# A short convolution on two 64-row halves, with a new order for the whole kernel

## The chip, the cores and the metric

One core of a Trainium2 chip. The metric is the time of one execution in microseconds on the device, the median of several runs. A run of the profiler gives one execution with its rows for every instruction; its span is the time from the first to the last of them, and its own time is a little more than the span.

The engines are TensorE (PE, with its weight loads PEld), VectorE (DVE), ScalarE (ACT), GpSimd (POOL) and SyncE (SP), which here only issues DMAs. All of them run their instructions in the order of the program.

## The reference

All inputs are bf16; one batch, S = 2048 positions, D = 640 channels, F = 1728.

```python
def A(q, k, v, shift_k, ssm_k, ssm_D):        # q is layernorm(x)
    k_shift = sum over t in 0..3 of  k_pad[:, t:t + S, :] * shift_k[:, 3 - t]
    kv = k_shift * v
    y = causal convolution of kv with ssm_k over all S positions, per channel   # by FFT
    return q * (y + kv * ssm_D)

x = A_q
h  = x + A(layernorm(x), A_k, A_v, A_shift_k, A_ssm_k, A_ssm_D)
h2 = h + (silu(n @ w_gate) * (n @ w_up)) @ w_down     # n = layernorm(h)
```

So every position of k is mixed with the three before it, channel by channel ("taps"), then comes the long convolution, then a gated feed-forward net.

## The kernel before

The positions are cut into four blocks of 512. Position p * 4 + r of a block lies in partition p and "row" r (R = 4 rows of 128 partitions). Channels come in KT = 5 chunks of 128. The long convolution is done with a transform of length 1024 per block: matrices WF (forward, L345 in `forward`) and WI (inverse, L703 in `inverse`) on TensorE, and products of spectra on VectorE (`mac`, L560 for a first product, L587 and L588 for those that add). Block j takes the spectra X0..Xj of kv and the windows H0..Hj of the filter, whose spectra are called G. The result is multiplied with the normalized x and added (L717, L723), normalized again (L598, L645, L648), turned (L743 and copies L745, or a transposing DMA L736) and given to the feed-forward net `ffn` of that block: gate and up projections (L789 and L824), silu and product (L807 to L834), down projection (L856), and the store.

The short convolution, where the change lies: k of block 0 is loaded plainly (L506) and turned on TensorE by `turned_k` (L519, with copies L521 by ScalarE or VectorE), k of the others by transposing DMAs (L508). After that, channels lie in the partitions. In `kv_of`, for each row r, TensorE runs 20 pairs of weight load and matmul (L540): 5 chunks times 4 taps, the weights being turned k (128 channels by 128 positions) and the moving operand a diagonal matrix of 128 columns with that tap of the channels. The four sums of a row lie in PSUM in the layout of v. For block 0 VectorE multiplies with v straight out of PSUM (L545, four products of 640 columns); for the others ScalarE copies (L547) and VectorE multiplies in place (L548), or VectorE does both at once. The matrix `diag`, 20 diagonals of 128 columns, is made by one VectorE product (L892) from the identity and the loaded taps `tapw` (L882 in the rows of SP's issues).

The order of all work on each engine is fixed ahead by a planner, `Plan`. Each operation has an engine, a cost in nanoseconds, its reads and writes, and a priority. The planner takes the operations as its own model of time lets them start, those of lower priority number first. The priority of each stage is a base (10 for each block) plus an offset of the table PLACE: "k1" is the short convolution of block 1, "X1" its transform, "m11" a product, "f0" a feed-forward block, "Lk1", "Lv1", "Lg1", "Lx1" are loads, "LWF", "LWI", "Lm" (the table of negatives for the transforms, "minus"), "Ld", "Lw1" (`wd`, the weights of the down projection) and "Lwg" (the first feed-forward weights) too. SP's loads are one queue in the order of the plan. Buffers are few: SLOTS gives one for x, two for `ld` (v and g, which take turns in the order of their creation), two for `kT` (k), eight for spectra.

Of the kernel before, what the change touches and what calls it, by code (L numbers as in the profile page):

```python
# [19 lines left out]
P = 128  # L20
# [4 lines left out]
EPS = 1e-5  # L25
NEWTON = ((1.68191274, 0.70395035), (1.50000037, 0.50000005))
KT = D // P
NC_FULL = 13
NCH = NC_FULL + 1
NGRP = 7  # L30
NH = 320
ADDLO, ADDMAC, ADDWIN, ADDH, LEAD = ('G1',), (), (), (2,), {}
PAD = 16
DIRECT, ACTLN, ACTKV, ACTLN2 = ('inv0', 'G0', 'G1'), 1, 1, (2, 3)
LN1DVE, LN2POOL, HTURN = (2,), (), (2, 1)
GTURN = (3, 1, 2)
SUM = {'i3': 'four', 'G1': 'four', 'X1': 'four', 'X0': 'four'}
ADDP = {(3, 2): ((0, 1),), (2, 2): ((0, 1),), (2, 1): ((0, 0),)}
WAIT = {'dve': 450, 'act': 450, 'pe': 150}
PLACE = {"G0": 26.0, "G1": -15.5, "G2": -8.0, "G3": 12.0, "LWF": -13.5, "LWI": 16.0, "Ld": 20.0, "Lg0": -24.0,  # L40
# [8 lines left out]
SLOTS = {"S": 8, "scr": 4, "x": 1, "ld": 2, "kT": 2, "t4": 2, "hT": 1, "tT": 1, "wgu": 2, "row": 3, "o": 2,  # L49
         "sg": 2, "ps_c": 2, "ps_f": 2, "sm": 6}  # L50
SPLIT = ((0,), (1,))
# [36 lines left out]
class Plan:  # L88
# [4 lines left out]
    def __init__(self, slots, in_turn=()):  # L93
        self.ops, self.slots = [], slots
        self.turn = {t: [] for t in in_turn}
        self.at = {}
        self.all = 0.0

    def line(self, block, name, at, **own):

        at += PLACE.get(name, 0.0)
        self.block, self.all, self.at = block, at, {e: p + PLACE.get(name + e, 0.0) for e, p in own.items()}

    def add(self, eng, ns, fn, reads=(), writes=(), holds=(), other=None):


        deps, bufs = set(), list(holds)
        for acc, is_w in [(a, False) for a in reads] + [(a, True) for a in writes]:
            b, part = acc if isinstance(acc, tuple) else (acc, None)
            if b not in bufs:  # L110
                bufs.append(b)
            for op, p2, w2 in b.log:
                if (is_w or w2) and (part is None or p2 is None or part == p2
                                     or isinstance(part, frozenset) and isinstance(p2, frozenset) and part & p2):
                    deps.add(op)
        op = Op(len(self.ops), eng, ns, fn, self.at.get(eng, self.all), bufs, deps)
        op.other = other
        for acc, is_w in [(a, False) for a in reads] + [(a, True) for a in writes]:
            b, part = acc if isinstance(acc, tuple) else (acc, None)
            b.log.append((op, part, is_w))  # L120
        for b in bufs:
            b.left += 1
        self.ops.append(op)
        return op

    def schedule(self):
# [10 lines left out]
        while todo:  # L137
            found = []
            for op in todo:
                ready = 0.0  # L140
                ok = True
                want = {}
                for b in op.bufs:
                    if b.tag is not None and b.at is None:
                        if b.tag in self.turn and self.turn[b.tag][0] is not b:
                            ok = False
                            break
                        n = want[b.tag] = want.get(b.tag, 0) + 1
                        if len(idle[b.tag]) < n:
                            ok = False  # L150
                            break
                        ready = max(ready, sorted(idle[b.tag])[n - 1][0])
                    elif b.tag is not None:
                        ready = max(ready, b.since)
                if not ok:
                    continue
                for way, late in [((op.eng, op.ns, op.fn), 0.0)] + ([(op.other, 1e3)] if op.other else []):
                    at = max(ready, free.get(self.QUEUE.get(way[0], way[0]), 0.0))
                    for d in op.deps:
                        if d.eng != way[0] or d.eng in self.ISSUE:  # L160
                            at = max(at, d.end + self.LAND.get(d.eng, 0))
                    found.append(((at, op.prio + late, op.n), op, way))
            best = min(found, key=lambda f: f[0]) if found else None
            if best:
                until = best[0][0] + WAIT.get(best[2][0], 0)
                best = min((f for f in found if f[2][0] == best[2][0] and f[0][0] <= until and (f[0][1] <= best[0][1] - 5 or f is best)),
                           key=lambda f: (f[0][1] // 5, f[0][0], f[0]))
            assert best is not None, "the plan is stuck"
            (start, _, _), op, way = best
            if way is op.other and op.rest:  # L170
                op.rest.ns, op.rest.fn = 0, None
# [33 lines left out]
def kernel(ctx: ExitStack, tc: tile.TileContext, A_q, A_k, A_v, A_shift_k, A_ssm_k, A_ssm_D, B_x,  # L205
# [80 lines left out]
    WF = fixed([P, R, 4, P], BF16, "WF")  # L286
    WI = fixed([P, 4, R, P], BF16, "WI")
    tapw = fixed([P, KT, 4], BF16, "tapw")
    diag = fixed([P, KT * 4, P], BF16, "diag")
    wd = fixed([P, NCH, D], BF16, "wd")  # L290
    blanks = Buf(None)

# [209 lines left out]
    def load_k(j):  # L502

        kT = new("kT")
        if j == 0:
            load(MB, lambda: nc.sync.dma_start(out=plain(kT), in_=block(kk, j)), [kT])  # L506
        for r in range(R) if j else ():
            plan.add("turn", MB / 4 / 300.0, lambda r=r: nc.sync.dma_start(  # L508
                out=ap(kT)[:, :, r, PAD:], in_=block(kk, j)[:, r, :], transpose=True), [], [(kT, r)])
        return kT  # L510

    def turned_k(k):
        kT = new("kT")
        for r in range(R):
            pt = conv_ps()

            def tr(r=r, pt=pt):
                for c in range(KT):
                    nc.tensor.transpose(turned(pt)[:, c * P:(c + 1) * P], plain(k)[:, r, c * P:(c + 1) * P], ap(ident))  # L519
            pe(290, tr, [k, ident], [pt], [kT])  # L520
            evict(lambda copy, r=r, pt=pt: copy(  # L521
                ap(kT)[:, :, r, PAD:], turned(pt)[:, 0:D].rearrange("p (c t) -> p c t", c=KT)), [pt], [(kT, r)], other=490)
        return kT
# [1 line left out]
    def kv_of(j, kT, before, v):  # L525
# [4 lines left out]
            plan.add("pool", 900, lambda: nc.gpsimd.tensor_copy(ap(kT)[:, :, :, PAD - 1:PAD], ap(before)[:, :, :, PAD + P - 1:]),  # L530
                     [(before, r) for r in range(R)], [(kT, "halo")])
        kv = new("t4")
        for r in range(R):
            ps = conv_ps()

            def mm(r=r, ps=ps):
                for c in range(KT):
                    for t in range(4):
                        q, off = (r - t, PAD) if r >= t else (r - t + 4, PAD - 1)
                        nc.tensor.matmul(line(ap(ps))[:, c * P:(c + 1) * P], ap(kT)[:, c, q, off:off + P],  # L540
                                         ap(diag)[:, 4 * c + t, :], start=(t == 0), stop=(t == 3))
            pe(1130, mm, [kT, diag], [ps], [kv])

            def straight(r=r, ps=ps):
                nc.vector.tensor_mul(ap(kv)[:, r, :], line(ap(ps)), rd(v)[:, r, :])  # L545
            if plan.block >= ACTKV:
                op = plan.add("act", 700, lambda r=r, ps=ps: nc.scalar.copy(ap(kv)[:, r, :], line(ap(ps))), [ps, v], [(kv, r)], (), ("dve", 820, straight))  # L547
                op.rest = dve(490, lambda r=r: nc.vector.tensor_mul(ap(kv)[:, r, :], ap(kv)[:, r, :], rd(v)[:, r, :]), [v], [(kv, r)])  # L548
            else:
                dve(820, straight, [ps, v], [(kv, r)])  # L550
        return kv

    def mac(A, X, H, first, pieces=((0, 1),), adds=()):
# [23 lines left out]
        for xs, hs, dst, f in ((0, 0, 0, nc.vector.tensor_add), (0, 1, 1, nc.vector.tensor_add),  # L577
# [1 line left out]
            b = new("scr")  # L579

            if (xs, hs) in adds:
                dve(1490, lambda b=b, xs=xs, hs=hs: nc.vector.tensor_mul(flat2(b), X.part(xs), H.part(hs)), [X.at(xs), H.at(hs)], [b], [A.b])
                add_into(lambda dst=dst: A.part(dst), lambda b=b: flat2(b), [b], [A.at(dst)])
                continue

# [162 lines left out]

    def load_w(gi):
        w = new("wgu")  # L750
        was = plan.all
        if plan.block == 0 and gi < 2:
            plan.all = PLACE.get("Lwg", 5.0)
        f0 = gi * 2 * P

        def cols(src, lo, n):
# [5 lines left out]
        for i, (to, src, lo, n) in enumerate(parts):  # L762
            load(P * KT * n * 2, lambda to=to, src=src, lo=lo, n=n: nc.sync.dma_start(
                out=ap(w)[:, :, to:to + n], in_=cols(src, lo, n)), [(w, i)])
        plan.all = was
        return w

    def ffn(j, hT, h, end=False, lead=0):
# [110 lines left out]
    def first(name, at):  # L879
        plan.line(0, name, at)  # L880
    first("load", 0.0)
    load(1e3, lambda: nc.sync.dma_start(out=ap(tapw), in_=A_shift_k.rearrange("(c p) t -> p c t", p=P)), [tapw])  # L882
    dve(100, lambda: nc.vector.memset(ap(ident), 1.0), [], [ident])
    plan.add("pool", 700, lambda: nc.gpsimd.affine_select(ap(ident), ap(ident), [[-1, P]], ALU.is_equal, 0.0, base=0, channel_multiplier=1), [], [ident])

    def blank():
        nc.gpsimd.memset(ap(wd)[64:P, NC_FULL, :], 0.0)
        for t in place["tT"]:
            nc.gpsimd.memset(t[64:P, NC_FULL, :], 0.0)
    plan.add("pool", 2000, blank, [], [blanks])  # L890
    k = load_k(0)
    dve(2800, lambda: nc.vector.tensor_mul(  # L892
        ap(diag), ap(ident).unsqueeze(1).to_broadcast([P, KT * 4, P]),
        ap(tapw).rearrange("p c t -> p (c t)").unsqueeze(2).to_broadcast([P, KT * 4, P])), [ident, tapw], [diag])
    first("Lx0", 0.1)
    x = load_x(0)
    first("Lv0", 0.2)
# [127 lines left out]
```

## Time and profile before

| | us |
|---|---|
| median of 3 runs (lowest, highest) | 282.18 (281.87, 284.87) |
| the profiled execution | 282.56 |
| its span | 280.8 |
| TensorE busy | 260.9 |
| VectorE busy | 207.0 |
| ScalarE busy | 175.6 |
| HBM read and written | 30.01 MB and 4.59 MB |

A row of the page names a line of the kernel, an engine and an operation, then the written and read tiles with their shapes; behind the bar stand busy time and the mean of one in nanoseconds, then the idle time ahead of them and who ended it. The chain of waits is followed back from the last instruction: at each step to what released it. Matmuls are pipelined, and the row of one lasts longer than its spacing to the next; the number of matmuls by the stretch that they take is the better reading.

### The profile page before, as it was taken

What the parts mean: (1) busy time and instruction counts of PE and PEld (TensorE: products, weight loads), DVE (VectorE), ACT (ScalarE), POOL (GpSimd) and SP (SyncE); (2) the same over time, 40 slices, a digit from 0 to 9 for tenths busy, and PEclk for the clock granted to TensorE, in tenths of its full rate; (3) what the DMA queues carried; (4) which work ended last, traced back from release to release, by engine and by line L of the source; (5) the groups of instructions that cost most, each with busy time, mean ns of one, the idle gap of its engine ahead of it and who ended that gap; (6) DMA issues with size and microseconds to landing.
All of it is one profiled execution on the core that took longest, in us unless ns stands there. A gap on an engine that the chain in (4) does not pass through costs nothing.

```text
span 280.8 us, 4663 instructions
## 1 busy us (share of the span) xinstructions
PE 260.9 (93%) x1787; PEld 162.0 (58%) x1804; DVE 207.0 (74%) x294; ACT 175.6 (63%) x285; POOL 52.8 (19%) x71
## 2 busy tenths in 40 slices
PE   0699989899999999999999999998989999999994
PEld 0686766645456677965545567643435774444672
DVE  0568996988999988899998999999999630011211
ACT  5547746998896877487756886386348643454300
POOL 2030100000398001131003101234950121000000
PEclk9999999999999999999999999999999999999999
DMA  7999992289957734959557495859545244653011
GB/s 251 338 366 237 240 233 98 93 194 250 258 118 92 216 122 101 170 83 205 143 141 150 98 245 85 174 117 232 148 102 152 27 47 86 170 154 59 0 49 48
DMA packets 74553, 42.77 MB, mean 152 GB/s; under 512 B 34145, under 2 KB 71842, under 8 KB 74530
## 3 DMA queue, kind: packets, MB, share of 16 engines
q1 hardware_dynamic: 71410, 37.88, 53.2%
q0 software_dynamic: 3120, 4.59, 11.6%
q8 instruction: 14, 0.23, 0.3%
q14 instruction: 9, 0.07, 0.1%
HBM read 30.01 MB, written 4.59 MB: 123 GB/s over the span
## 4 chain that ended last, share of the span: by engine, by line
PE 68%; DVE 16%; DMA 6%; ACT 6%; issue 2%; SPq 0%; DVEq 0%; ACTq 0%
PE ps_f L789 26%; PE ps_f L856 16%; PE ps_c L345 8%; PE ps_c L703 6%; DVE scr L587 5%; DVE S L588 5%; PE ps_c L540 5%; PE ps_f L824 4%; DMA kT<-in_A_k_dram 2%; DMA ld<-in_A_ssm_k_dram 2%; DMA wgu<-in_B_w_gate_dram 2%; ACT S L334 2%; DVE S L560 1%; PE ps_f L540 1%; ACT sg L807 1%
## 5 line engine op out<-in xcount | busy, mean ns | idle before, releaser
L789 PE MATMUL ps_f<-hT,wgu 128*128 128x512 bf16 x465 | 106.6, 379 | 3.3 <-ACT sg L807 2.3
L789 PEld LDWEIGHTS <-wgu 128*128 128x128 bf16 x480 | 46.7, 98 | 56.2 <-issue 2.8
L856 PE MATMUL ps_f<-wd,tT 128*128 128x320 bf16 x448 | 63.5, 299 | 0.1
L856 PEld LDWEIGHTS <-tT 128*128 128x128 bf16 x448 | 43.7, 98 | 17.2 <-issue 0.4
L807 ACT ACTIVATE sg<-ps_f 128x1024 bf16<-128x1024 f32 (+1 forms) x28 | 27.0, 963 | 24.6 <-PE ps_f L789 12.5
L815 DVE TENSOR_TENSOR tT<-sg,sg 128x1024 bf16<-128x1024 bf16 (+1 forms) x27 | 17.5, 647 | 27.4 <-ACT sg L813 27.4
L345 PE MATMUL ps_c<-t,WF 128*128 128x320 bf16 x208 | 34.9, 299 | 0.6 <-ACT S L334 0.5
L813 ACT CAST sg<-ps_f 128x1024 bf16<-128x1024 f32 (+1 forms) x27 | 25.6, 950 | 14.5 <-PE ps_f L789 14.5
L588 DVE TENSOR_TENSOR S<-S,scr 128x2560 bf16<-128x2560 bf16 x21 | 31.4, 1493 | 0.7
L587 DVE TENSOR_TENSOR scr<-S,S 128x2560 bf16<-128x2560 bf16 x21 | 31.2, 1485 | 0.3 <-DMA S<-scr 0.2
L345 PEld LDWEIGHTS <-WF 128*128 128x128 bf16 x240 | 23.4, 98 | 13.2 <-issue 1.5
L598 ACT ACTIVATE row<-x 128x640 bf16<-128x640 bf16 x32 | 23.4, 733 | 5.5 <-DVE x L723 5.1
L862 POOL DMA_DIRECT2D out_dram<-o x12 | 10.6, 883 | 70.7 <-ACT o L861 70.7
L334 ACT CAST S<-ps_c 128x640 bf16<-128x640 f32 (+1 forms) x31 | 18.9, 622 | 7.0 <-PE ps_c L345 6.4
L540 PEld LDWEIGHTS <-kT 128*128 128x128 bf16 x320 | 20.1, 103 | 2.3 <-issue 0.8
L540 PE MATMUL ps_c<-diag,kT 128*128 128x128 bf16 x280 | 17.7, 223 | 0.7 <-DVE hT L745 0.7
L648 ACT ACTIVATE row<-x,sm 128x640 bf16<-128x640 bf16 x17 | 15.0, 919 | 2.7 <-DMA x<-row 1.3
L637 ACT ACTIVATE row<-x 128x640 bf16<-128x640 bf16 x16 | 11.7, 731 | 7.5 <-DMA x<-in_A_q_dram 7.5
L703 PEld LDWEIGHTS <-WI 128*128 128x128 bf16 x128 | 12.4, 98 | 6.8 <-issue 1.2
L861 ACT CAST o<-ps_f 128x640 bf16<-128x640 f32 x12 | 8.2, 687 | 10.8 <-PE ps_f L856 10.8
L717 DVE SCALAR_TENSOR_TENSOR row<-row,ps_c 128x640 bf16<-128x640 bf16 x14 | 11.5, 819 | 3.7 <-PE ps_c L703 3.6
L824 PE MATMUL ps_f<-hT,wgu 128*128 128x512 bf16 x58 | 13.8, 379 | 0.1
(105 smaller groups left out, 293.6 us busy)
## 6 DMA issues: line engine op xcount, KB each, us to landing
wgu<-in_B_w_gate_dram SPq DMA_DIRECT2D x24, 320.0 KB, 3.5
wgu<-in_B_w_up_dram SPq DMA_DIRECT2D x24, 320.0 KB, 3.6
x<-in_A_q_dram SPq DMA_DIRECT2D x4, 640.0 KB, 3.8
ld<-in_A_v_dram SPq DMA_DIRECT2D x4, 640.0 KB, 5.8
ld<-in_A_ssm_k_dram SPq DMA_DIRECT2D x4, 640.0 KB, 5.3
wd<-in_B_w_down_dram SPq DMA_DIRECT2D x1, 2080.0 KB, 12.0
out_dram<-x SPq DMA_DIRECT2D x3, 640.0 KB, 3.6
out_dram<-o POOLq DMA_DIRECT2D x12, 160.0 KB, 3.5
```

Of the source, the lines that this page charges most:

```text
L334: (lambda: nc.scalar.activation(dst(), src(), ACT.Copy, scale=2.0)) if twice else (lambda: nc.scalar.copy(dst(), src())),
L345: nc.tensor.matmul(ap(ps)[:, h, 0:NH], w, ap(src)[:, r, h * NH:(h + 1) * NH], start=(first and i == 0), stop=(last and i == len(rs) - 1), ...
L540: nc.tensor.matmul(line(ap(ps))[:, c * P:(c + 1) * P], ap(kT)[:, c, q, off:off + P], ap(diag)[:, 4 * c + t, :], start=(t == 0), stop=(t == 3))
L587: nc.vector.tensor_mul(flat2(b), X.part(xs), H.part(hs))
L588: f(A.part(dst), A.part(dst), flat2(b))
L598: act(930, lambda r=r, junk=junk: nc.scalar.activation(ap(junk), ap(x)[:, r, :], ACT.Square, scale=D ** -0.5, accum_out=sm(s, 1)[:, r:r + ...
L703: nc.tensor.matmul(ap(ps)[:, w, 0:NH], m, src[:, w * NH:(w + 1) * NH], start=(i == 0), stop=(i == len(terms) - 1))
L789: nc.tensor.matmul(of(ps, i), ap(w)[:, k, off:off + P], ap(hT)[:, k, lo:lo + n], start=(k == 0), stop=(k == KT - 1))
L807: act(1010 if wide else 600, lambda: nc.scalar.activation(of(sg), of(*gate), ACT.Silu), [(gate[0], gate[1] + i) for i in range(m)], [sg])
L813: op = plan.add("act", 1010 if wide else 590, lambda: nc.scalar.copy(of(co), of(*up)), psu + [sg], [co] + tt, (), ("dve", 1230 if wide els ...
L824: nc.tensor.matmul(ap(ps)[:, i, :], ap(w)[:, k, off:off + P], ap(hT)[:, k, :], start=(k == 0), stop=(k == KT - 1))
L856: nc.tensor.matmul(ap(ps)[:, hf, 0:NH], ap(tT)[:, c, at:at + P], ap(wd)[:, c, hf * NH:(hf + 1) * NH], start=(c == order[0]), stop=(c == or ...
```

## The change

1. *Taps.* The channels of a chunk are split in two halves of 64 partitions. `diag` has 64 columns for each diagonal, and both halves of it are the same 64 columns (from `eye`, the sum of the left and right halves of the identity: ones where the column is the channel modulo 64). For each chunk and half there are seven matmuls with 64 partitions in place of 16 with 128: the weights are one row q of the turned k, and the moving operand takes all diagonals that this row is needed for, 64 to 256 columns. The two halves alternate and write to two PSUM banks. PSUM is taken by groups of chunks, (0, 1), (2, 3) and (4), not by rows: five reads of 512 columns. In blocks 1 to 3 ScalarE copies them, and one VectorE product over the whole block multiplies with v; in block 0 VectorE multiplies out of PSUM five times.
2. *Start.* k of block 0 is loaded in two halves, and its transposes wait for their half alone. By the new places x, the taps and k are the first loads. 24 matmuls of the identity with itself are added ("warm"), written to a PSUM buffer that nobody reads.
3. *Plan.* A table HOLD gives the DMAs of some stages an earliest time in the planner's model (no wait at run time), every stage can have a place per engine, and all of PLACE is new. In `mac`, a product that is to be added by DMA now also depends on the part of A that it will be added to.

```diff
-PLACE = {"G0": 26.0, "G1": -15.5, ...
+PLACE = {"G0": 64.8, "G1": -70.4, "G2": -11.7, "G3": -15.2, "LWF": 1.2, "LWI": 68.9, "Ld": 43.3, "Lg0": -15.6, "Lg1":
+         14.3, "Lg2": 11.0, "Lg3": 14.2, "Lk0": -36.1, "Lk1": 80.0, ... "Lm": 79.3,
+         "Lt": -71.4, "Lv0": 0.1, ... "Lw1": -25.7, "Lwg": -63.8, "Lx0":
+         -76.7, ...
+HOLD = {"LWI": 23000, "Lg1": 24500, "Lg2": 28500, "Lk1": 18000, "Lk2": 51500, "Lk3": 78500, "Lm": 16500, "Lv1": 10500,
+        "Lv2": 46000, "Lw1": 86000, "Lwg": 34500, "Lx1": 10500, "Lx2": 104500, "Lx3": 124000, "f2": 128000,
+        "f3": 97000, "g3": 20000, "i2": 1500, "m12": 44000, "m22": 20500, "m23": 38000, "t2": 3000}
...
-                ready = 0.0
+                ready = op.hold
...
-    diag = fixed([P, KT * 4, P], BF16, "diag")
+    diag = fixed([P, KT * 4, HALF], BF16, "diag")
+    eye = fixed([P, HALF], BF16, "eye")
...
         if j == 0:
-            load(MB, lambda: nc.sync.dma_start(out=plain(kT), in_=block(kk, j)), [kT])
+            for lo in (0, 2):
+                load(MB // 2, lambda lo=lo: nc.sync.dma_start(out=plain(kT)[:, lo:lo + 2], in_=block(kk, j)[:, lo:lo + 2, :]), [(kT, ("in", lo // 2))])
...
-            pe(290, tr, [k, ident], [pt], [kT])
+            pe(290, tr, [(k, ("in", r // 2)), ident], [pt], [kT])
...
-        for r in range(R):
+
+        def taps(cs, ps):
+            for i, c in enumerate(cs):
+                runs = [(q, PAD, q, R, 0) for q in range(R)] + [(q, PAD - 1, 0, q, R - q) for q in range(1, R)]
+                for n, (q, off, lo, hi, t) in enumerate(runs):
+                    for h in range(2):
+                        ch = slice(h * HALF, (h + 1) * HALF)
+                        nc.tensor.matmul(ap(ps)[:, h, (i * R + lo) * HALF:(i * R + hi) * HALF], ap(kT)[ch, c, q, off:off + P],
+                                         ap(diag)[ch, R * c + t:R * c + t + hi - lo, :], start=(n == 0), stop=(n == len(runs) - 1), skip_group_check=True)
...
+        for cs in ((0, 1), (2, 3), (4,)):
             ps = conv_ps()
...
+            pe(440 * len(cs), lambda cs=cs, ps=ps: taps(cs, ps), [kT, diag], [ps], [kv])
+            for hs in ((0,), (1,)) if len(cs) == 2 else ((0, 1),):
...
+                if plan.block >= ACTKV:
+                    act(600, lambda cs=cs, hs=hs, src=src: nc.scalar.copy(by_half(ap(kv), cs, hs), src()), [ps, v], [(kv, (cs, hs))])
+                else:
+                    dve(690, lambda cs=cs, hs=hs, src=src: nc.vector.tensor_mul(by_half(ap(kv), cs, hs), src(), by_half(rd(v), cs, hs)), [ps, v], [kv])
+        if plan.block >= ACTKV:
+            dve(1490, lambda: nc.vector.tensor_mul(ap(kv), ap(kv), rd(v)), [v], [kv])
...
-                dve(1490, lambda b=b, xs=xs, hs=hs: nc.vector.tensor_mul(flat2(b), X.part(xs), H.part(hs)), [X.at(xs), H.at(hs)], [b], [A.b])
+                dve(1490, lambda b=b, xs=xs, hs=hs: nc.vector.tensor_mul(flat2(b), X.part(xs), H.part(hs)), [X.at(xs), H.at(hs), A.at(dst)], [b], [A.b])
...
+    def warm():
+        for _ in range(WARM):
+            nc.tensor.matmul(ap(idle)[:, 0, 0:P], ap(ident), ap(ident), start=True, stop=True)
+    pe(110 * WARM, warm, [ident], [idle])
+    first("diag", 0.0)
+    dve(200, lambda: nc.vector.tensor_add(ap(eye), ap(ident)[:, 0:HALF], ap(ident)[:, HALF:P]), [ident], [eye])
+    dve(1490, lambda: nc.vector.tensor_mul(
+        ap(diag), ap(eye).unsqueeze(1).to_broadcast([P, KT * 4, HALF]),
+        ap(tapw).rearrange("p c t -> p (c t)").unsqueeze(2).to_broadcast([P, KT * 4, HALF])), [eye, tapw], [diag])
```

More of the change, by code (lines that the diff above doesn't have):

```diff
@@ L27 @@
 KT = D // P
+HALF = P // 2
 NC_FULL = 13
@@ L33 @@
 PAD = 16
+WARM = 24
 DIRECT, ACTLN, ACTKV, ACTLN2 = ('inv0', 'G0', 'G1'), 1, 1, (2, 3)
@@ L39 @@
 WAIT = {'dve': 450, 'act': 450, 'pe': 150}
-PLACE = {"G0": 26.0, "G1": -15.5, "G2": -8.0, "G3": 12.0, "LWF": -13.5, "LWI": 16.0, "Ld": 20.0, "Lg0": -24.0,
[8 rows of a table removed]
+PLACE = {"G0": 64.8, "G1": -70.4, "G2": -11.7, "G3": -15.2, "LWF": 1.2, "LWI": 68.9, "Ld": 43.3, "Lg0": -15.6, "Lg1":
[9 rows of a table added]
+HOLD = {"LWI": 23000, "Lg1": 24500, "Lg2": 28500, "Lk1": 18000, "Lk2": 51500, "Lk3": 78500, "Lm": 16500, "Lv1": 10500,
+        "Lv2": 46000, "Lw1": 86000, "Lwg": 34500, "Lx1": 10500, "Lx2": 104500, "Lx3": 124000, "f2": 128000,
+        "f3": 97000, "g3": 20000, "i2": 1500, "m12": 44000, "m22": 20500, "m23": 38000, "t2": 3000}
 SLOTS = {"S": 8, "scr": 4, "x": 1, "ld": 2, "kT": 2, "t4": 2, "hT": 1, "tT": 1, "wgu": 2, "row": 3, "o": 2,
@@ L96, in __init__ @@
         self.at = {}
-        self.all = 0.0
+        self.all = self.hold = 0.0
     def line(self, block, name, at, **own):
         at += PLACE.get(name, 0.0)
-        self.block, self.all, self.at = block, at, {e: p + PLACE.get(name + e, 0.0) for e, p in own.items()}
+        self.hold = HOLD.get(name, 0.0)
+        self.block, self.all = block, at
+        self.at = {e: own.get(e, at) + PLACE.get(name + e, 0.0) for e in ("pe", "act", "dve")}
     def add(self, eng, ns, fn, reads=(), writes=(), holds=(), other=None):
@@ L117, in add @@
         op.other = other
+        op.hold = self.hold if eng in self.ISSUE else 0.0
         for acc, is_w in [(a, False) for a in reads] + [(a, True) for a in writes]:
@@ L167, in schedule @@
                            key=lambda f: (f[0][1] // 5, f[0][0], f[0]))
-            assert best is not None, "the plan is stuck"
+            assert best is not None, f"the plan is stuck at {len(order)}"
             (start, _, _), op, way = best
@@ L532, in kv_of @@
         kv = new("t4")
-        for r in range(R):
-            ps = conv_ps()
[L536 to L550, printed above, removed]
+        def taps(cs, ps):
[6 more added lines that the diff above has]
+                                         ap(diag)[ch, R * c + t:R * c + t + hi - lo, :], start=(n == 0), stop=(n == len(runs) - 1), skip_group_check=True)
@@ new lines, in by_half, with src @@
+        def by_half(t, cs, hs):
+            v = t.rearrange("p r (c h i) -> p h c r i", c=KT, h=2)
+            return v[:, hs[0], cs[0]:cs[-1] + 1] if len(hs) == 1 else v[:, :, cs[0]]
+        for cs in ((0, 1), (2, 3), (4,)):
+            ps = conv_ps()
+            pe(440 * len(cs), lambda cs=cs, ps=ps: taps(cs, ps), [kT, diag], [ps], [kv])
+            for hs in ((0,), (1,)) if len(cs) == 2 else ((0, 1),):
+                def src(cs=cs, hs=hs, ps=ps):
+                    t = ap(ps).rearrange("p h (c r i) -> p h c r i", c=2, r=R)
+                    return t[:, hs[0]] if len(hs) == 1 else t[:, :, 0]
+                if plan.block >= ACTKV:
+                    act(600, lambda cs=cs, hs=hs, src=src: nc.scalar.copy(by_half(ap(kv), cs, hs), src()), [ps, v], [(kv, (cs, hs))])
+                else:
+                    dve(690, lambda cs=cs, hs=hs, src=src: nc.vector.tensor_mul(by_half(ap(kv), cs, hs), src(), by_half(rd(v), cs, hs)), [ps, v], [kv])
@@ L750, in load_w @@
         w = new("wgu")
-        was = plan.all
+        was = plan.all, plan.hold
         if plan.block == 0 and gi < 2:
             plan.all = PLACE.get("Lwg", 5.0)
+            plan.hold = HOLD.get("Lwg", 0.0)
         f0 = gi * 2 * P
@@ L764, in load_w @@
                 out=ap(w)[:, :, to:to + n], in_=cols(src, lo, n)), [(w, i)])
-        plan.all = was
+        plan.all, plan.hold = was
         return w
@@ L881 @@
     first("load", 0.0)
-    load(1e3, lambda: nc.sync.dma_start(out=ap(tapw), in_=A_shift_k.rearrange("(c p) t -> p c t", p=P)), [tapw])
     dve(100, lambda: nc.vector.memset(ap(ident), 1.0), [], [ident])
@@ L890 @@
     plan.add("pool", 2000, blank, [], [blanks])
+    first("Lk0", 0.01)
     k = load_k(0)
-    dve(2800, lambda: nc.vector.tensor_mul(
-        ap(diag), ap(ident).unsqueeze(1).to_broadcast([P, KT * 4, P]),
-        ap(tapw).rearrange("p c t -> p (c t)").unsqueeze(2).to_broadcast([P, KT * 4, P])), [ident, tapw], [diag])
+    first("Lt", 0.02)
+    load(1e3, lambda: nc.sync.dma_start(out=ap(tapw), in_=A_shift_k.rearrange("(c p) t -> p c t", p=P)), [tapw])
+    first("warm", 0.0)
+    idle = new("ps_f")
+    def warm():
[7 more added lines that the diff above has]
+        ap(tapw).rearrange("p c t -> p (c t)").unsqueeze(2).to_broadcast([P, KT * 4, HALF])), [eye, tapw], [diag])
     first("Lx0", 0.1)
```

17 rows, old and new, of the table PLACE are left out of this document.

## The prediction

> **What bounds the kernel now.** I read the head of the page first, then the busy time of each engine in the stretches that the chain of waits marks off. In the window rows the columns are the stretch, its length, the busy time of PE, PEld, DVE, ACT and POOL (with instruction counts), the granted clock, the DMA share and GB/s.
>
> ```profile
> span 280.8 us, 4663 instructions
> PE 260.9 (93%) x1787; PEld 162.0 (58%) x1804; DVE 207.0 (74%) x294; ACT 175.6 (63%) x285; POOL 52.8 (19%) x71
> PE 68%; DVE 16%; DMA 6%; ACT 6%; issue 2%; SPq 0%; DVEq 0%; ACTq 0%
> ```
>
> ```profile
> 0.00:8.78 8.78, 0.00 (x0) 0.00 (x0) 1.74 (x3) 4.27 (x9) 1.57 (x7) 1.00 0.78 279
> ...
> 61.50:163.00 101.50, 100.76 (x686) 61.19 (x695) 93.86 (x129) 77.45 (x126) 24.57 (x24) 1.00 0.73 157
> 163.00:205.00 42.00, 40.73 (x236) 23.00 (x237) 41.43 (x35) 25.13 (x41) 16.09 (x16) 1.00 0.74 165
> 205.00:232.45 27.45, 26.28 (x183) 17.14 (x184) 19.51 (x42) 16.52 (x26) 5.42 (x6) 1.00 0.38 73
> 232.45:277.00 44.55, 44.31 (x245) 23.99 (x245) 7.47 (x11) 15.16 (x17) 0.85 (x1) 1.00 0.34 85
> 277.00:280.80 3.80, 0.05 (x1) 0.00 (x0) 0.89 (x2) 0.00 (x0) 0.00 (x0) 1.00 0.15 45
> ```
>
> TensorE bounds it. Of its 280.8 - 260.9 = 19.9 us without work, 8.78 lie before its first instruction and 3.75 in the last stretch, so only 7.4 are scattered between. But VectorE is a close second: 93.86 + 41.43 = 135.3 us busy in the 143.5 us from 61.5 to 205, and from 163 to 205 it is the chain itself. From 232.45 only the last feed-forward block runs, 44.55 us of TensorE that nothing in this change touches. So the question is how much earlier that block can start.
>
> The beginning, as the chain and the timeline give it:
>
> ```profile
> 0.80 0.40 SPq L312 DMA_DIRECT2D x<-in_A_q_dram  x1
> 1.26 0.41 SPq L900 DMA_DIRECT2D WF<-const_wf  x1
> 1.72 0.43 SPq L882 DMA_DIRECT2D tapw<-in_A_shift_k_dram  x1
> 2.19 0.52 SPq L506 DMA_DIRECT2D kT<-in_A_k_dram  x1
> ...
> 7.23 2.83 DVE L892 TENSOR_TENSOR diag<-ident,tapw 128x2560 bf16<-128x2560 bf16 x1 [6.10 <-DMA tapw<-in_A_shift_k_dram]
> ...
> 18.99 0.43 PE L345 MATMUL ps_f<-t,WF 128*128 128x320 bf16 x2
> ```
>
> ```profile
> 2.19 6.55 DMA kT<-in_A_k_dram
> ...
> 8.79 0.71 PE ps_f L519 x5
> 9.50 0.53 PE ps_c L519 x5
> ...
> 11.69 2.21 PE ps_f L540 x19
> 13.90 1.68 PE ps_c L540 x20
> ```
>
> TensorE waits for k until 8.79, turns it in 20 transposes, runs the taps of block 0 (L540) from 11.69, and only at 18.99 reaches X0, the first transform (L345). Everything later hangs on that.
>
> **The loads at the head.** Before, x, WF (512 KB) and the taps are issued ahead of k. After, by the new places, SP's order is x, taps, k in two halves, v, g, WF: `ld` is given in turn, so v goes before g. The earliest times are used by the planner alone and do not delay an issue by themselves; they put WI, the minus table, wd and the early feed-forward weights behind k's and g's loads in SP's queue. WF's 524,288 bytes at the 279 GB/s of the first row are 1.9 us, so k should be complete near 8.78 - 1.9 = 6.9 us, its first half earlier. WF is now sixth, behind x, k, v and g: about 3.1 MB, 11 us at that rate; X0 must not need it earlier, and by the estimate below it doesn't. If X0 came sooner, WF would be what is late next. The second issue for k costs SP about 0.5 us (0.52 in the row of k) in front of v and g, which nobody awaits then.
>
> **diag.** 1280 elements in place of 2560 on VectorE: about half of 2.83, and `eye` beside it, together 1.7 us against 2.8. It is now ready when the taps have landed + 1.7; they are behind x alone, so this lies beside the wait for k. Worth nothing unless the taps land late; the former cover, 7.23 to 10.06, also ended ahead of the first matmul that needed all four rows of k.
>
> **The warm-up.** 24 matmuls of 128 columns need the identity only, and run while TensorE waits for k. What they may buy is in the same rows as a full-speed pair:
>
> ```profile
> 112.63 4.47 PE ps_c L540 x80
> ...
> 227.53 0.56 PE ps_c L743 x10
> ```
>
> Ten transposes take 0.56 us late in the kernel, 56 ns each; the first took 0.53 per five, 106 ns. The taps ran at 2.21/19 = 116 ns at first, against 4.47/80 = 56 later. At full speed the 20 transposes would save 20 x 50 = 1.0 us and the first 19 taps 19 x 60 = 1.1. The granted clock is 1.00 in every row, so it shows nothing of this; only the spacing does. The price of the warm-up is bounded by 24 x 106 = 2.5 us in a time when TensorE has nothing: free, unless it starts after k has landed. On this the Trainium skill (TensorE: Matmul & The Clock Gate, Part 1: The HAM clock gate) says that the full clock is given after a busy window of about 3.4 us, and lost after an idle one of that length. The slow spacing of the first transposes agrees. By that rule 2.5 us can be too short to turn the clock up; that is a rival below, with its price from the rows above.
>
> **The taps, all four blocks.** Before: 80 weight loads and 80 matmuls of 128 columns per block, 4.47 us. After: for each of 5 channel chunks seven runs on two halves of the rows, 14 loads and 14 matmuls, with (4+3+2+1+1+2+3) x 64 = 1024 columns per half. 70 pairs per block, and the same 10,240 columns if the halves follow one another, half of that in time if they run side by side. No 64-row matmul is in this trace, so I bound it from the nearest rows.
>
> ```profile
> 79.43 1.09 PE ps_c L345 x8
> ...
> L345 PE MATMUL ps_c<-t,WF 128*128 128x320 bf16 x208 | 34.9, 299 | 0.6 <-ACT S L334 0.5
> ...
> L540 PEld LDWEIGHTS <-kT 128*128 128x128 bf16 x320 | 20.1, 103 | 2.3 <-issue 0.8 <-DVE kT L521 0.7
> ```
>
> Eight matmuls of 320 columns in 1.09 us are 0.425 ns a column.
> - Side by side: 1024 x 0.425 = 0.44 us a chunk, 2.2 a block.
> - A pair no faster than the 56 ns of now: 70 x 0.056 = 3.9.
> - One after the other: 2 x 2.2 = 4.4.
> - Every weight load in the open: 70 x 0.103 = 7.2.
>
> The array also goes between 128-row and 64-row work: three groups a block, up to six edges. A matmul of 320 columns is spaced by 136 ns and lasts 299, so emptying the array costs at most 163 ns an edge, 1.0 us a block. The Trainium skill (TensorEngine Tiling (Array Packing), Key Properties) states that changing the tiling mode drains TensorE, which speaks against so small groups; no run here shows it yet. By it a block would be 2.2 + 1.0 = 3.2, without it 2.2. I take T = 2.7 us a block, half of the edges paid, nearest to the side-by-side row because neighbouring instructions always alternate between the halves, with a PSUM bank each (`ap(ps)[:, h, ...]`). Blocks 1 to 3 then save 3 x (4.47 - 2.7) = 5.3 us of TensorE.
>
> **What takes kv out of PSUM.**
>
> ```profile
> L547 ACT CAST t<-ps_c 128x640 bf16<-128x640 f32 x12 | 8.1, 697 | 1.7 <-PE ps_c L540 1.7
> L587 DVE TENSOR_TENSOR scr<-S,S 128x2560 bf16<-128x2560 bf16 x21 | 31.2, 1485 | 0.3 <-DMA S<-scr 0.2
> ...
> L813 ACT CAST sg<-ps_f 128x512 bf16<-128x512 f32 x4 | 2.3, 580 | 0.0
> ...
> L548 DVE TENSOR_TENSOR t<-t,ld 128x640 bf16<-128x640 bf16 x12 | 5.5, 486 | 0.9 <-ACT t L547 0.9
> ...
> L545 DVE TENSOR_TENSOR t<-ps_c,ld 128x640 bf16<-128x640 f32 x2 | 1.7, 826 | 1.0 <-PE ps_c L540 1.0
> ...
> L873 DVE TENSOR_TENSOR o<-ps_f,x 128x320 bf16<-128x320 f32 x2 | 0.9, 487 | 3.0 <-PE ps_f L856 3.0
> ```
>
> Blocks 1 to 3: ScalarE 5 x 0.58 = 2.9 for 4 x 0.697 = 2.8, the same; VectorE one product of 1.485 for 4 x 0.486 = 1.94, so 3 x 0.46 = 1.4 us less in all on the second bottleneck. Its price is that a transform of X can begin only after the whole product, about 1 us later than after a quarter; TensorE has feed-forward work there (100.76 of 101.5 busy), so nothing. Without that cover, 3 us. Block 0: five VectorE products of 512 columns, between the 0.826 of 640 and the 0.487 of 320: 0.69 each, 3.45 us in all for 3.3. The strided result is not in the trace; strides could raise it, but the runs are still 64 elements long.
>
> **The start, summed.** k at 6.9; turning and copying took 8.79 to 11.69, 2.9 us, now 2.4 with half of k there early; taps from 9.3; the first group of two chunks (0.9 to 1.1), then the five products behind one another, 3.45: X0 at 13.8. Before: 18.99. Gain **5.2 us**.
>
> **The rest.** On the path of TensorE: 5.2 + 5.3 = 10.5 us. On that of VectorE: 5.2 + 1.4 = 6.6. The second has slack at the end, which these rows show:
>
> ```profile
> 224.86 0.92 ACT L648 ACTIVATE row<-x,sm 128x640 bf16<-128x640 bf16 x1 [0.41 <-DVE sm L605]
> ```
>
> ```profile
> 227.37 0.72 PE L743 MATMUL ps_c<-ident,row 128*128 128x128 bf16 x10
> ```
>
> ```profile
> L745 ACT COPY hT<-ps_c 128x640 bf16<-128x640 bf16 x3 | 2.1, 694 | 0.9 <-PE ps_c L743 0.9
> ```
>
> The first rows of h3 were ready at 225.8, but TensorE turned them at 227.4 behind older work and began the last block at 232.45. With nothing in front of it, two pairs of rows, each 0.56 of transposes and 0.69 for a copy, would end at 228.3: 4.2 us of slack. Whether the slack can be used depends on the new order, and all of that is new: 70 places are changed. So the gain lies between 6.6 and 10.5; two engines over 93% busy seldom both keep theirs, and I take the middle, 8.6. The profiled execution took 282.56; 282.56 - 8.6 = 274.0. The median of the three runs, 282.18, is 0.4 below it: **273.6 us**. The new dependency on `A.at(dst)` orders VectorE behind its own older work and costs nothing by itself.
>
> **Rivals.** In general the path of TensorE changes by -5.2 + (T - 2.7) + 3 x (T - 4.47) = 4T - 21.3, with T the taps of a block.
> - *Halves one after the other, edges paid:* T = 4.4 + 1.0 = 5.4, change +0.3; without the edges -3.7. 278 to 282, no or little gain. For it: nothing in this trace overlaps two matmuls. Against: the alternation. 15%.
> - *Slower, because weight loads come into the open:* at T over 5.3 the whole gain is gone. With T = 7.2 it is +7.5, with edges 8.2 and +11.5: 289 to 294. For it: a load lasts 103 ns, and a 64-column matmul to hide it, at 0.425 ns a column, only 27. Against: 80 pairs in 4.47 us hide such loads behind 56 ns of work. 8%.
> - *The head gives its gain back:* the warm-up is too short, so transposes and taps stay slow (2.1 us), or a load that the order puts late (wd moves behind the early blocks; it is 2 MB) stops TensorE for 3 to 5 us, or the VectorE path alone counts with part of its gain. For it: 70 new places and one queue, in which a blocked load holds all behind it. Against: SP's longest wait now, by its own row, is for feed-forward weights whose buffers TensorE still reads, 98.2 us in 39 times, and only 0.2 us of it ever reached a matmul. 276 to 281. 14%.
>
> ```profile
> SPq L763 <- PE ps_f L789: 98.2, 39, 19.8
> ```
>
> ```profile
> PE ps_f L789 <- DMA wgu<-in_B_w_gate_dram: 0.2, 1, 0.2
> ```
>
> - *More than forecast:* the order takes part of the 7.4 us of scattered idle time too, and both paths get their full 10.5: 264 to 269. 13%.
>
> **Numbers.** Forecast 270 to 277: 50%. A measurement of this kernel can tell about 1% from no change, so faster means below 279.4, slower above 285. Faster 0.77 (50 + 13, some 9 of the 14, a third of the 15), same 0.14, slower 0.09. The range 265 to 283 leaves out the slower rival and the far end of the better case.
>
> **What would show it.** TensorE's first transpose of k near 7 us with 56 ns spacing; X0 at 13 to 14.5; L540's successor at 2.2 to 3.2 us a block (70 instructions); the last feed-forward block starting at 222 to 226 and still lasting 44.5. Wrong if taps take over 5 us a block, if TensorE's idle time between first and last instruction grows past 10 us, or if VectorE is idle more than now between 61 and 205.

## The result and the profile after

The changed kernel takes 272.78 us (272.41 to 273.20 in 4 runs), the kernel before 283.52 in the runs beside it: a ratio of 0.962, 95% interval 0.955 to 0.970. The forecast was 273.6. The executions of the kernel before came in two groups, near 282 and near 285, so this median lies above the 282.18 that the forecast started from. The profiled execution took 272.41. The head of its page:

```profile
span 270.7 us, 4631 instructions
PE 256.1 (95%) x1773; PEld 153.9 (57%) x1788; DVE 204.9 (76%) x288; ACT 175.5 (65%) x287; POOL 56.6 (21%) x71
PE 58%; DVE 24%; ACT 9%; DMA 4%; issue 3%; SPq 0%; DVEq 0%; ACTq 0%
```

The same stretches as before, each from the same event (columns as in the prediction):

```profile
153.00:195.00 42.00, 41.76 (x243) 23.72 (x244) 40.18 (x43) 28.04 (x46) 19.01 (x18) 1.00 0.78 170
195.00:222.31 27.31, 26.52 (x185) 17.24 (x185) 19.90 (x42) 17.16 (x26) 5.46 (x5) 1.00 0.39 76
222.31:267.00 44.69, 44.35 (x244) 23.95 (x245) 7.52 (x12) 15.15 (x17) 0.85 (x1) 1.00 0.34 85
267.00:270.70 3.70, 0.00 (x0) 0.00 (x0) 0.83 (x2) 0.00 (x0) 0.00 (x0) 1.00 0.16 47
```

The last feed-forward block lasts as long as before (44.69 for 44.55) and starts at 222.31 for 232.45: all of the gain, 10.1 us, comes ahead of it. The start, from the timeline of the changed kernel:

```profile
1.72 0.99 SPq L517 DMA_DIRECT2D kT<-in_A_k_dram  x2
...
2.31 2.74 PE L919 MATMUL ps_f<-ident 128*128 128x128 bf16 x24 [2.31 <-POOL ident L903]
...
4.63 1.49 DVE L923 TENSOR_TENSOR diag<-eye,tapw 128x1280 bf16<-128x1280 bf16 x1 [2.15 <-DMA tapw<-in_A_shift_k_dram]
...
6.66 0.71 PE L530 MATMUL ps_f<-ident,kT 128*128 128x128 bf16 x5 [1.60 <-DMA kT<-in_A_k_dram]
...
8.91 2.06 PE L551 MATMUL ps_f<-diag,kT 64*128 64x256 bf16 x28
...
14.49 0.43 PE L355 MATMUL ps_c<-t,WF 128*128 128x320 bf16 x2
...
20.78 0.38 SPq L310 DMA_DIRECT2D ld<-in_A_ssm_k_dram  x1
```

X0 comes at 14.49 for 18.99. More telling is the last of these rows, the load of g1, the filter of block 1. In the kernel before, the same load and ScalarE's reordering copy of what it brings (`g_turned`, "scr<-ld") stand in the timeline so:

```profile
13.80 0.43 SPq L940 DMA_DIRECT2D wd<-in_B_w_down_dram  x1
14.28 3.49 SPq L942 DMA_DIRECT2D wd<-in_B_w_down_dram  x1
17.88 9.04 SPq L508 DMA_TRANSPOSE kT<-in_A_k_dram  x4
27.03 0.53 SPq L300 DMA_DIRECT2D ld<-in_A_ssm_k_dram  x1
```

```profile
32.98 2.56 ACT L415 COPY scr<-ld 128x2560 bf16<-128x2560 bf16 x1 [1.62 <-DMA ld<-in_A_ssm_k_dram]
```

and in the changed kernel:

```profile
13.50 6.56 SPq L519 DMA_TRANSPOSE kT<-in_A_k_dram  x4
```

```profile
26.56 2.61 ACT L425 COPY scr<-ld 128x2560 bf16<-128x2560 bf16 x1 [0.23 <-issue]
```

The copy is 6.4 us earlier, more than the 4.5 of X0. SP no longer issues wd's 2.2 MB ahead of k1 and g1. ScalarE works in the order of the program, so until this copy has its data the copies of kv1 behind it wait too (L547), and then TensorE's inverse transform (L703). The chain of the kernel before has these steps in a row:

```profile
27.03 5.88 DMA ld<-in_A_ssm_k_dram
32.98 2.56 ACT scr L415
35.54 0.60 ACT t L547
36.18 1.25 PE ps_c L703 x8
```

### The profile page after: what moved, and what is told of

Read it like the earlier page. It is cut to its first block, busy times and chain, and to the rows that moved or that the text cites. A ratio compares the mean times of both kernels' runs of the same rounds, so it can differ in the third digit from the quotient of the medians.

```text
span 270.7 us, 4631 instructions
## 1 busy us (share of the span) xinstructions
PE 256.1 (95%) x1773; PEld 153.9 (57%) x1788; DVE 204.9 (76%) x288; ACT 175.5 (65%) x287; POOL 56.6 (21%) x71
## 4 chain that ended last, share of the span: by engine, by line
PE 58%; DVE 24%; ACT 9%; DMA 4%; issue 3%; SPq 0%; DVEq 0%; ACTq 0%
PE ps_f L809 23%; PE ps_f L876 17%; DVE scr L606 6%; PE ps_c L355 6%; DVE S L607 6%; PE ps_c L722 4%; PE ps_f L844 3%; ACT sg L827 2%; DMA ld<-in_A_ssm_k_dram 2%; DVE S L579 2%; DMA kT<-in_A_k_dram 2%; DVE tT L835 2%; ACT S L344 2%; ACT sg L833 1%; DVE S L390 1%
## 5 line engine op out<-in xcount | busy, mean ns | idle before, releaser
L344 ACT CAST S<-ps_c 128x640 bf16<-128x640 f32 (+1 forms) x31 | 18.3, 622 | 4.5 <-PE ps_c L355 4.0
L667 ACT ACTIVATE row<-x,sm 128x640 bf16<-128x640 bf16 x18 | 16.0, 917 | 4.4 <-DVE x L742 1.9
L344 ACT ACTIVATE scr<-ps_c 128x640 bf16<-128x640 f32 (+1 forms) x20 | 12.6, 657 | 2.7 <-PE ps_c L355 2.5
L579 DVE TENSOR_TENSOR S<-S,S 128x2560 bf16<-128x2560 bf16 (+1 forms) x10 | 11.9, 1217 | 0.3 <-ACT S L344 0.2
## 6 DMA issues: line engine op xcount, KB each, us to landing
wd<-in_B_w_down_dram SPq DMA_DIRECT2D x1, 2080.0 KB, 10.1
```

Source lines behind the costliest of these rows:

```text
L344: (lambda: nc.scalar.activation(dst(), src(), ACT.Copy, scale=2.0)) if twice else (lambda: nc.scalar.copy(dst(), src())),
```

## Experiments

The edits of runs 1, 4 and 6 and the last one of run 8 change only the sequence of SP's issues, in the finished plan; the order on every other engine stays as it was. All ratios are to the kernel before on the same chip, where its median lay between 282.6 and 283.5. A difference between two changed kernels can be one between chips as well; the kernel before alone differs by 0.9 us so.

**1. The start alone.**

```diff
 order = plan.schedule()
+order.remove(wf)
+order.insert(order.index(g0) + 1, wf)
```

> The kernel before, with one load moved: WF is issued behind g, as in the changed kernel; the order of every other instruction is kept. Theory A (the step of the prediction): k lands about 1.9 us earlier, near 6.9; X0 moves from 19.0 to about 17.1, and the end follows: 280.3 us for 282.2. Theory B: TensorE and VectorE catch up on nothing, the gain is lost in later waits: X0 earlier, end within 0.5 us of before. Theory C: WF, now sixth, is what X0 waits for, and X0 itself moves by less than 0.5.

284.11 us; ratio 1.002 (0.999 to 1.006). k landed at 8.0 for 8.8 and X0 came at 18.0, one microsecond earlier, not 1.9; the end did not follow. ScalarE's row shows why: the copy of g1 started where it had.

```profile
33.24 2.54 ACT L415 COPY scr<-ld 128x2560 bf16<-128x2560 bf16 x1 [2.84 <-DMA ld<-in_A_ssm_k_dram]
```

ScalarE only waits longer in front of it, 2.84 us for 1.62. TensorE stood longer as well, and its granted clock fell for a while in this execution (a window row of this run):

```profile
36.00:42.00 6.00, 5.58 (x29) 3.45 (x29) 3.24 (x8) 1.79 (x4) 0.00 (x0) 0.72 1.04 239
```

**2. Cheaper taps alone, and with the start.** In `kv_of`:

```diff
-                    for t in range(4):
+                    for t in range(2):
```

> The kernel before, with the taps t = 2 and 3 left out: 40 pairs a block for 80, everything else in the same order, so TensorE has 2.2 us less per block, about what the 64-row halves save. Theory A (the path of TensorE sets the end): 3 x 2.2 = 6.7 from blocks 1 to 3 and 2 to 3 at the start, 273 to 274 us. Theory B (the path of VectorE sets it): only the start counts, 279 to 280 us. The middle that the prediction took lies between.

> The kernel before with both edits, WF behind g and half of the taps left out, in the old order of all else. If the new places add nothing of their own, this comes to the time of the changed kernel, 272 to 273 us, or below it. If the new places carry part of the gain, it stays above 275.

282.73 us, ratio 1.000 (0.997 to 1.003), and 283.14 us, 1.002 (0.999 to 1.005). TensorE lost 160 pairs and 7.4 us of busy time (253.5 for 260.9), X0 came at 16.2 and 15.3, and nothing was gained at the end: both theories of mine fell. In the run with both edits the mean granted clock was below 1.00 in every execution (0.984 to 0.994), so a part of what it saved may have gone there; with half the taps alone the profiled execution had 1.00 throughout and took 282.54. The copy of g1, first with half the taps, then with both edits:

```profile
33.71 2.47 ACT L415 COPY scr<-ld 128x2560 bf16<-128x2560 bf16 x1 [4.88 <-DMA ld<-in_A_ssm_k_dram]
```

```profile
32.28 2.52 ACT L415 COPY scr<-ld 128x2560 bf16<-128x2560 bf16 x1 [4.38 <-DVE S L560]
```

The last row names a product of VectorE, but the copy does not need it: in the kernel before it started at 32.98, ahead of the same product (34.92). What is left is the load of g1, issued at 27.52 and taken up 4.8 us later; in the three kernels ahead of this one it was 5.3 to 6.0.

**3. The new code with the old places.** PLACE of before, HOLD empty.

> The changed kernel with the old table of places and no earliest times, so the planner makes another order. Theory A (the taps pay by themselves, the places only order the loads at the head): 6 us of taps and 1 to 2 at the start, 274 to 276 us. Theory B (the order of all work is what was gained): 279 us or more.

345.55 us, ratio 1.223 (1.220 to 1.226). The numbers of the table were made for the other costs; with them TensorE stands for 35.9 us in one place:

```profile
PE ps_c L719 <- DVE scr L680: 35.9, 1, 35.9
```

This says that the table belongs to the code, and nothing on the taps: the run does not decide between its two theories.

**4. wd out of the way.** The new theory is that g1's landing was the gate in the old order.

```diff
 order = plan.schedule()
+order = [op for op in order if op not in downs]      # the two loads of wd
+at = order.index(turn1) + 1                          # the last transpose of g1
+order[at:at] = downs
```

> The kernel before with the two loads of wd (2.1 MB) moved on SP's queue, from ahead of the transposing loads of k1 to behind the transposes of g1; the order of all else kept. New theory (the landing of g1 is the gate: ScalarE's reordering copy of g1 started at 33.0, 33.2, 33.7 and 32.3 us in the kernel before and in its variants with a faster start or cheaper taps, against 26.6 in the changed kernel): with wd out of the way the copy starts by 28 and the end comes 3 to 6 us earlier, 276 to 279 us. Rival (the order of VectorE's own work holds the end): the copy starts earlier, the end stays within 1 us of before.

281.20 us, ratio 0.993 (0.990 to 0.996): a little faster, less than I had expected, though more than the rival allowed. SP came to g1 at 19.9 for 27.0, and the copy started without a wait for it, but only at 31.36:

```profile
31.36 2.60 ACT L415 COPY scr<-ld 128x2560 bf16<-128x2560 bf16 x1
```

Now ScalarE's own earlier work, the copies of X0 and G0, ends last; it takes some 12 us from X0 (19.01) on. So there were two gates in a row, 1.6 us apart, and opening one shows the other. In the changed kernel the two end together: its chain has the load land at 26.33, and ScalarE's copies end at 26.34, again 12 us after X0.

**5. wd, WF and the taps together; then the taps of block 0 alone.**

> The kernel before with wd late, WF behind g, and the taps t = 2 and 3 left out. New theory (g1 was the gate that hid both parts): copy of g1 at 26 to 27 us, 271 to 274 us, the time of the changed kernel without its places. Rival (the new order of all engines is needed): 278 us or more.

277.06 us, ratio 0.979 (0.975 to 0.983). That lies between the two theories, and the copy of g1 came at 28.3, not at 26 to 27. Still, the two parts that gave nothing alone give 4.1 us more than wd alone, 5.9 us together with it. Then with all 80 pairs back in blocks 1 to 3:

> The kernel before with wd late and WF behind g, and the taps t = 2 and 3 left out in block 0 alone; blocks 1 to 3 keep all 80 pairs. It parts the two terms of the prediction, the start (5.2 us) and the taps of blocks 1 to 3 (5.3 us). Theory A (VectorE's chain carries the gain from the copy of g1 to the end, TensorE has room for the taps): the copy of g1 at 28 as with half the taps everywhere, 277 to 278.5 us. Theory B (TensorE's work in blocks 1 to 3 counts in full once g1 is out of the way): 280 us or more.

278.38 us, 0.982 (0.977 to 0.987). The two copies of g1, with half the taps everywhere and in block 0 alone:

```profile
28.32 2.62 ACT L415 COPY scr<-ld 128x2560 bf16<-128x2560 bf16 x1
```

```profile
28.43 2.59 ACT L415 COPY scr<-ld 128x2560 bf16<-128x2560 bf16 x1
```

So the start with its loads, wd's among them, is worth some 4.5 us, and 6.7 us of TensorE's taps in blocks 1 to 3 only some 1.3: Theory A. The intervals of the two ratios overlap, so the 1.3 is not certain by the medians; the last column of the table below gives 1.5.

**6. The reverse, in the changed kernel.** wd's loads put ahead of k1's.

> The changed kernel with the reverse edit: the two loads of wd ahead of the transposing loads of k1. New theory: the copy of g1 moves from 26.6 to 31 us or later and the end follows by 3 to 6 us, 276 to 279 us. Rival: the copy moves, the end by less than 1 us, 272.5 to 273.7 us.

278.92 us, ratio 0.985 (0.981 to 0.989): as the new theory had it, 6.1 us of the gain are gone by two loads in another place of one queue.

```profile
33.36 2.48 ACT L425 COPY scr<-ld 128x2560 bf16<-128x2560 bf16 x1 [7.07 <-DMA ld<-in_A_ssm_k_dram]
```

X0 still came at 14.45. The granted clock fell here too (0.61 and 0.54 from 28 to 36), but the way from the copy to the last block is as long as in the changed kernel, so the whole shift was there before the copy. Where the gate opens and where the last block starts, in the profiled executions, with the median of all executions of each kernel:

| kernel | X0 | copy of g1 | last feed-forward block | from copy to block | median us |
|---|---|---|---|---|---|
| before | 18.99 | 32.98 | 232.3 | 199.3 | 282.2 |
| WF behind g | 18.02 | 33.24 | 234.4 | 201.1 | 284.1 |
| half taps | 16.21 | 33.71 | 231.7 | 198.0 | 282.7 |
| both | 15.29 | 32.28 | 230.5 | 198.2 | 283.1 |
| wd late | 19.01 | 31.36 | 231.6 | 200.2 | 281.2 |
| wd late, WF, half taps in block 0 | 15.84 | 28.43 | 228.3 | 199.9 | 278.4 |
| the same, half taps everywhere | 14.85 | 28.32 | 226.7 | 198.4 | 277.1 |
| changed | 14.49 | 26.56 | 222.2 | 195.6 | 272.8 |
| changed, wd early | 14.45 | 33.36 | 228.9 | 195.6 | 278.9 |

The last block follows the copy of g1, not X0: the way between them is 195.6 us in the new order, 198.0 to 198.4 in the old one with half the taps everywhere, and 199.3 to 200.2 with all of them in blocks 1 to 3 (201.1 where the clock fell behind the copy). Of the 10.1 us that the profiled execution gained, 6.4 lie ahead of this copy and 3.7 behind it.

**7. How the halves run.** The two loops of `taps` exchanged:

```diff
-                for n, (q, off, lo, hi, t) in enumerate(runs):
-                    for h in range(2):
+                for h in range(2):
+                    for n, (q, off, lo, hi, t) in enumerate(runs):
```

> The changed kernel with the two loops of the taps exchanged: all seven matmuls of one half, then all seven of the other, so that neighbours on TensorE share their rows except once a chunk. Theory A (the halves overlap because neighbours alternate): a block of taps goes from 2.4 to about 4.5 us, the kernel to 279 to 281 us. Theory B (the saving is in fewer and wider matmuls, not in overlap, or the array overlaps them in any order): 2.4 us a block as before, 272.8 us.

274.20 us, ratio 0.969 (0.965 to 0.974), 1.4 us more than the changed kernel; the intervals overlap, but the way from the copy of g1 to the last block grew by 1.6 us as well, to 197.2. Four chunks, first alternating, then in turn, with the row that follows each, and a single chunk, from the timelines of the two kernels:

```profile
25.76 1.95 PE L551 MATMUL ps_c<-diag,kT 64*128 64x256 bf16 x56
27.65 0.72 PE L722 MATMUL ps_f<-S,WI 128*128 128x320 bf16 x4
...
34.61 0.62 PE L551 MATMUL ps_c<-diag,kT 64*128 64x256 bf16 x14
35.16 2.08 PE L722 MATMUL ps_c<-S,WI 128*128 128x320 bf16 x14
```

```profile
25.71 2.48 PE L551 MATMUL ps_c<-diag,kT 64*128 64x256 bf16 x56
28.13 0.72 PE L722 MATMUL ps_f<-S,WI 128*128 128x320 bf16 x4
...
34.75 0.88 PE L551 MATMUL ps_c<-diag,kT 64*128 64x256 bf16 x14
35.57 1.67 PE L722 MATMUL ps_c<-S,WI 128*128 128x320 bf16 x11
```

Alternating, four chunks take 1.89 and one 0.55: 2.44 a block. Three more chunks cost 1.34, so a chunk is 0.447 and what a stretch of such work pays besides is 0.10. 2048 columns in 0.447 us are half of 0.425 ns each: the halves run side by side. In turn a block takes 2.42 + 0.82 = 3.24, not 4.5: Theory A was wrong in size, for the halves overlap in part even so. The trace shows how: 0.3 us after the start five matmuls have begun, and two of them have 256 columns. So the second half's first matmul, the eighth in the program, has begun ahead of three of the first half's seven. (Each half of a chunk has one matmul of 256 columns, its first.) What lets it is open.

**8. The head of the changed kernel.** 0 or 42 warm-up matmuls for 24, and x's load behind k's:

```diff
-        for _ in range(WARM):
+        for _ in range(42):      # the other run: range(0)
...
+order.remove(x0)
+order.insert(order.index(k0) + 1, x0)
```

> The changed kernel without the 24 warm-up matmuls, the order of all else kept. Theory A (they end at 4.9, TensorE is idle until 6.66, and the first transposes are slow all the same, so they buy nothing): within 0.4 us of 272.8. Theory B (they bring forward the moment at which the spacing halves, 11.5 us in the changed kernel): that moment comes at 12.5 or later, X0 1 to 1.5 us later, 274 to 274.5 us.

> The changed kernel with 42 warm-up matmuls for 24, the order of all else kept: at 107 ns they last from 2.3 to 6.8, up to the landing of k. Theory A (TensorE needs some microseconds of unbroken work): the spacing halves by 7 to 8 us, transposes or taps of block 0 go at the fast spacing, X0 comes 1 to 1.5 us earlier, 271.3 to 271.8 us. Theory B (no effect of what runs before k): 272.8, or 0.2 more where the last of them stand before k.

> The changed kernel with x issued behind the two halves of k instead of ahead of the taps, the order of all else kept. Theory A (k sets the start): its first half lands about 2 us earlier, near 4.7, X0 moves from 14.5 to 12.5, and the end follows, 270.8 us. Theory B (g, WF or the sums of the first normalization on ScalarE, which need x, are late next): X0 moves by less than 0.7 us, 272.1 to 273 us.

Without: 272.47 us, ratio 0.963 (0.960 to 0.967), no difference to the 24; Theory A. With 42: 271.87 us, 0.961 (0.958 to 0.965), the lowest median of all, though its interval overlaps that of the changed kernel. The transposes went fast from the third group on, and X0 came at 13.69:

```profile
7.30 0.74 PE L530 MATMUL ps_c<-ident,kT 128*128 128x128 bf16 x5
7.83 0.50 PE L530 MATMUL ps_f<-ident,kT 128*128 128x128 bf16 x5
8.17 0.44 PE L530 MATMUL ps_c<-ident,kT 128*128 128x128 bf16 x5
```

k ahead of x: 273.23 us, 0.966 (0.962 to 0.971). k landed at 4.8, 1.8 us earlier, and X0 came at 13.97: now ScalarE, whose sums need x, is late with the copies of g0.

```profile
13.97 0.69 PE L355 MATMUL ps_c<-t,WF 128*128 128x320 bf16 x2 [1.29 <-ACT t L440]
```

Theory B, but the run does not tell what half a microsecond of X0 is worth. It was lost on the way to the copy of g1, which came at 26.94 for 26.56: behind that pause each group of two pairs took 0.53 us for 0.27 until 16.6, and the granted clock read 0.65 from 12 to 16.

## Why the prediction was right, and where it was not

**The time was right, its cause only in part.** 273.6 was forecast, 272.78 measured; the last block was to start at 222 to 226 and started at 222.3. But the sum was of two gains, 5.2 at the start and 5.3 in the taps, and the runs show that in the old order neither exists by itself. That the number came out so well is in part luck: the new order held a move that the sum did not have, and the taps gave less than their term.

**The step that failed: "Everything later hangs on that", on X0.** In the old order it hung on g1's landing, 14 us later; with that out of the way it hung on X0 again, through ScalarE's 12 to 13 us of copies. The landing was in the chain of waits before (5.88 us of DMA at 27.03, with the copy and the inverse transform behind it), and I gave it no price. The prediction names the load of wd only as a danger of the new order; moving it was the condition of the gain, worth 6.1 us in the changed kernel (run 6): 272.78 with it, 278.92 without, X0 the same.

**The loads at the head.** k was to be complete near 6.9, and its first half was turned from 6.66. As a single edit in the old order WF gave k 0.8 us, not 1.9, so the rate of the first window is no rate for one load among others.

**The taps.** T was set at 2.7 and measured 2.44: side by side as forecast, the edges 0.10 a stretch and not up to 0.33. The Trainium skill's rule that a change of tiling mode drains TensorE (TensorEngine Tiling (Array Packing), Key Properties) fits these 0.10 us, but no run here shows that they are a drain. Three blocks save 3 x (4.47 - 2.44) = 6.1 us of TensorE. Their worth was mis-sized: some 1.3 us for 6.7 in the old order; some 1.4 lost for 3 x 0.8 = 2.4 given back in the new one. TensorE is busy 95% of the span, but in the changed kernel the chain of waits runs mostly through VectorE from 87 to 131 us, where the taps of block 3 lie (104.6 and 122.9); those of block 2 are on it. That this is why the taps count so little is read from the chain; no run parts it from other reasons.

```profile
78.55 1.88 PE ps_c L551 x56
...
111.12 1.50 DVE S L607
```

**Evictions and diag.** 0.684 a product (0.69), ScalarE 0.590 (0.58), VectorE 1.483 (1.485). diag was ready at 6.1, ahead of k. VectorE's busy time fell by 2.1 us.

**The warm-up.** The rival held: 24 were too few, the transposes still took 0.53 per five, and X0 came at 14.5 instead of 13.8. The price at the end was under 1 us, not 2.1, by run 8. It is not so in every execution: in run 6, with the same 24, the transposes went at 0.29 per five from 7.08 on and slowed again after 8.2, and X0 came no earlier.

**The middle between 6.6 and 10.5** was a choice without a mechanism. In the old order wd's move, the start and the taps together give 5.9 us; the remaining 4.3, from 277.06 to 272.78, came with the new order and VectorE's shorter work. No run parts those two. By the table 1.8 us of it lie ahead of the copy of g1 and 2.8 behind. Where behind is open: from 100 to 160 us VectorE was idle 4.4 us with the old order and 2.5 with the new, but from 60 to 200 it was 7.1 and 6.4.

```profile
100.00:160.00 60.00, 58.92 (x373) 35.18 (x377) 55.56 (x86) 42.90 (x72) 9.52 (x10) 1.00 0.73 154
```

```profile
100.00:160.00 60.00, 58.57 (x400) 34.48 (x403) 57.48 (x74) 42.58 (x70) 9.52 (x10) 1.00 0.73 163
```

The first row is of the kernel with wd late, WF behind g and half the taps everywhere, the second of the changed one.

## What to carry to other kernels

Where every engine follows a fixed order, a saving can end at the next gate: walk the chain of waits past the first event and price each DMA on it before adding gains up. A big load that nobody needs for 80 us can hold back one that is needed now, in the same queue; look at what stands ahead of each late load. And move single issues in a finished plan to test this: the planner's numbers, changed, make another kernel.

## What the runs showed of the hardware

- Matmuls on two halves of the rows run side by side: 56 of them, 8192 columns, in 1.89 us. The Trainium skill (TensorE: Matmul & The Clock Gate, Part 3: Packing small matmuls) says that tiles in different row groups run at the same time; the trace agrees. The same part of the Trainium skill says that matmuls start and end in the order of the program, by which I would expect half after half to overlap only at the seam. There the trace differs: a matmul of the second half began ahead of three of the first, and a block took 3.24 us where two times 2.2 would be 4.4.
- The spacing of TensorE's matmuls halved after 5.6 us of work without a pause from 2.3 on (run with 42), and near 6.4, 4.1 us after the start, in the run with k ahead of x. In these two the profile's clock stood at 1.00 throughout the slow part, so it doesn't show the first rise. Later falls do show, as 0.72 in run 1, 0.65 in the run with k ahead of x and 0.54 in run 6. A pause need not bring one: with half the taps TensorE worked 0.96 of the 4 us from 32 to 36, and behind that eight matmuls of 320 columns took 1.10 us, for 2.02 in run 1.
- SP took 9.04 us for four transposing loads behind wd, 6.06 with wd moved and nothing else (run 4) and 6.56 in the changed kernel: a load can be late because of the time that the issues ahead of it take.
